# Attention two batches ahead of the output, with two batches in float32 beside the preparation of w_in

## The chip, the core and the metric

The kernel runs on one core of a Trainium2 chip. The metric is the device time of one launch in microseconds (us). A core has five engines that each work through their own queue in order: TensorE (PE; its weight loads are listed apart as PEld), VectorE (DVE), ScalarE (ACT), GpSimd (POOL) and SyncE (SP), which here issues all the DMAs. They wait for one another by semaphores. PE writes only into PSUM, which this kernel cuts into eight banks under the names `psc` (2 tiles of 2 banks), `pm` (3 tiles) and `pav` (1 tile).

## The reference

Sigmoid attention feeds a two-layer network with an ELU between its layers.

```python
# q, k, v: (8, 12, 448, 64) float32; w_in: (768, 2048); w_out: (2048, 768)
S = q.shape[2]
scores = np.matmul(q, k.transpose(0, 1, 3, 2)) / np.sqrt(64) - np.log(S)
attn = 1.0 / (1.0 + np.exp(-scores))
attn_out = np.matmul(attn, v).astype(np.float32)
x = attn_out.transpose(0, 2, 1, 3).reshape(8 * 448, 768)
h = x @ w_in
g = np.where(h > 0.0, h, np.exp(np.minimum(h, 0.0)) - 1.0)
out = (g @ w_out).astype(np.float32)
```

The two weights arrive as 8-byte floats, so that each weight is two 32-bit words.

## The kernel before

**Split numbers.** Most matmuls multiply float32 values that are held as two float16 values, a high part and a low part. `split` (lines 120 to 122) makes them: ACT writes the high part, scaled by a power of two, and DVE subtracts it from the source to get the low part. A product then takes three float16 matmuls: high by high, low by high, high by low. The scale of a tile is found first: DVE reduces the largest magnitude of each partition (`absmax`, line 125), multiplies an identity matrix by it (`dg`, line 105), PE multiplies that by ones to spread it over all partitions (`pb`, line 110), and DVE and POOL turn the result into scales (lines 112 to 114 and 317 to 327). `prepare` makes the reductions and `dg`, its inner `scales` makes `pb` and the scales, and `transposed` makes the splits of q and k (`nat`), of v (`vn`), and the DMA that transposes `nat` into `qk` (line 352). They run as three steps, which the main loop calls `second` (what `prepare_pair` returns) and `third` (what `second` returns).

**Attention.** The work goes batch by batch (8), and in a batch by pairs of heads (6). The class `Pair` holds a pair's four key tiles (three of 128 keys for each of two heads, and a rest tile with 64 keys of both). `scores` multiplies keys by queries into `psc`; `soften` applies the sigmoid on ACT into `sg` and splits it into `at` (ACT line 413, DVE line 414); `values` multiplies by v into `pav`; `finish` splits `pav` into `xh`, the attention output of the pair, and takes its largest magnitude. `EXACT = 1` says that batch 0 does its attention in plain float32: no splits of q, k, v and the sigmoid, but seven PE transposes for each pair (line 337), a copy to `early` (line 341), and float32 matmuls.

**Weights.** w_in is read in 16 tiles. `w_in_tile` finds the power of two of each from its words (ACT lines 138 and 142, DVE lines 143 and 157, sums on PE line 150) and splits it into `wi` (lines 121 and 122). The list `W_IN` says how many tiles have been done after each pair. w_out is read by `load_w_out` in 2 halves of 16 tiles: 16 magnitude steps of a half, then its 16 splits. A part of the staging lies in buffers that attention uses (`at`, `o`). `step` advances this by one tile; `wo` takes the place of the staging of w_in, so that it can start only when all of w_in is split.

**Hidden layer and output.** `hidden(b)` first calls `rescale`, which brings the six pairs of x to one scale (lines 448 to 452: five DVE instructions on whole `xh` tiles), and then `moe1`: 16 groups of 18 matmuls into `ph`, each followed by the exponential on ACT (line 511), the ELU on DVE (513, 514) and a split into `g`. `moe2(b)` multiplies `g` by `wo`: 48 matmuls for each tile of the output, 6 tiles for an even batch and 8 for an odd one (an odd batch also takes the last 64 tokens of the batch before), with a scaled copy `o` on DVE and a DMA out.

**Order.** The part up to and with `hidden(0)` is ordered by a scheduler, which may interleave what it finds ready: batch 0's pairs beside the w_in tiles, then `moe1` of batch 0 beside w_out (`w_out_beside`: four steps for each f from 2). The rest stands under `manual_schedule` for PE, ACT, DVE and SP, in the order of the code: for b = 1 to 7, attention of batch b with the matmuls of `moe2(b - 1)` filled in (`fill`: between the first two and the last two score tiles, and again before `values`), then `hidden(b)`. In pair n the splits of pair n + 1 (`third`) come after its first two softened tiles, the maxima of pair n + 2 (`prepare_pair`) before its last two, and the scales of pair n + 2 (`second`) ahead of `values`. Behind the last `hidden` stands `moe2(7)` alone. ACT changes between the sigmoid's and the exponential's tables once each way in a batch, and manual dependencies keep that so.

Of the kernel before, what the change touches and what calls it, by code (L numbers as in the profile page):

```python
# [32 lines left out]
def attention_ffn(  # L33
# [12 lines left out]
    P = 128  # L46
# [10 lines left out]
    EXACT = 1  # L57
    SP = 4
    SKEW = 2
    W_IN = [1, 3, 6, 9, 12, 15, 16]  # L60
    W_LOAD = [1, 1]
    W_OUT = 4
# [180 lines left out]
    last_exp = {}  # L243
# [123 lines left out]
    class Pair:  # L367
# [23 lines left out]
        def soften(self, g):  # L391
# [6 lines left out]
            if b - 1 in last_exp:  # L398
                tc.add_manual_dep(
                    a.ins,  # L400
                    last_exp[b - 1],
# [41 lines left out]
    def rescale(b, xh, xs):  # L443
# [5 lines left out]
        for c in range(NP - 1):  # L449
            nc.vector.tensor_scalar(xh[:, c], xh[:, c], rr[:, c : c + 1], None, op0=ALU.mult)  # L450
        nc.vector.tensor_tensor(
            xm[:, : NP - 1], xm[:, : NP - 1], rr[:, : NP - 1], op=ALU.mult
        )
        yield
# [24 lines left out]
    def moe1(b, g, xh, m, first, beside=None):  # L479
# [8 lines left out]
        for f in range(NF):  # L488
# [23 lines left out]
            last_exp[b] = a.ins.name  # L512
            nc.vector.tensor_scalar(e, e, 1.0, -1.0, op0=ALU.min, op1=ALU.add)  # L513
# [82 lines left out]
    def prepare_pair(n):  # L596
# [4 lines left out]
        if hp == 0:  # L601
            xh_of[b] = sb.tile([P, NK, 2, S], F16, tag="xh", name=f"xh{b}", bufs=2)
            xs_of[b] = sb.tile([P, 3, NP], F32, tag="xs", name=f"xs{b}", bufs=2)
# [11 lines left out]

    def w_out_beside(f):
        nonlocal wo, steps
        if f == 0:
            w_in_ratios()
            wo = sb.tile([P, NH, NF, 2, HM], F16, tag="wo", name="wo")  # L620
            steps = load_w_out(wo)
        if f >= 2:
            step(W_OUT)
        if f == NF - 1:
            step(1)
# [5 lines left out]
    def hidden(b, beside=None):  # L631
# [3 lines left out]
        next(whole)  # L635
        yield
# [38 lines left out]
    third = prepare_pair(EXACT * NP + 1)()  # L675
# [3 lines left out]
    next(h)  # L679
# [5 lines left out]
    with tc.manual_schedule(engines={E.PE, E.Activation, E.DVE, E.SP}):  # L685
        for b in range(EXACT, B):
            out_scale(*of_moe2, slice(0, 1 if b == EXACT else NH))
            tiles = moe2(b - 1, g, wo)
            left = NF * NH * (NC + (b - 1) % 2)
# [7 lines left out]
            for hp in range(NP):  # L697
                n = b * NP + hp
                share = left // (NP - hp)
                tail = 4 if hp == NP - 1 else 0  # L700
# [4 lines left out]
                third()  # L705
# [15 lines left out]
                fill(share - gap - tail)  # L721
                third = second()
# [3 lines left out]
                fill(tail)  # L726
# [3 lines left out]
        out_scale(*of_moe2)  # L730
        for _ in moe2(B - 1, g, wo):
            pass
# [30 lines left out]
```

## Time and profile before

| | |
|---|---|
| device time, median of 3 runs | 1272.22 us (1271.79 to 1273.72) |
| the profiled execution's own time | 1270.86 us |
| its span, first to last instruction | 1269.1 us |
| PE busy | 1200.2 us (95%), 7246 matmuls |
| DVE busy | 823.4 us (65%), 1872 instructions |
| ACT busy | 671.8 us (53%), 1015 instructions |
| POOL busy | 84.1 us (7%), 319 instructions |
| mean granted TensorE clock | 0.984 |
| HBM read, written | 58.20 MB, 11.01 MB |

The span is what the trace covers. The profiled execution's own time is 1.76 us longer, and it lies 1.36 us below the median of the runs. A busy PE isn't PE at its peak: the matmuls are pipelined and their ends are modelled. In a timeline a row is a run of like instructions: start, time from the first start to the last end, engine, line, operation, output and input tiles, shapes, count, and in brackets the idle time ahead of it with what ended it. Line numbers in all rows are those of the kernel before, unless the changed kernel is named; there most lines are 1 to 21 higher.

### The profile page before, as it was taken

To read this page: it belongs to the slowest core of one execution; us is meant where nothing else is said; L and a number is where in the kernel's file an instruction comes from. 1 tells how busy PE (TensorE), PEld (TensorE's weight loads), DVE (VectorE), ACT (ScalarE), POOL (GpSimd) and SP (SyncE) were. 2 spreads that over 40 slices of the span, in tenths; PEclk is the share of its full clock that TensorE was granted. 3 is DMA by queue.
4 is the path that set the end of the run, shared out by engine and by line. 5 is a ranking of instruction groups with operands and counts; after the bars stand their busy time and mean duration, and the time that the engine had idled before them with its cause. 6 is when DMAs were issued, how large, how long until landed. Compare 5 with 4: busy or idle time off the path is not lost.

```text
span 1269.1 us, 19337 instructions
## 1 busy us (share of the span) xinstructions
PE 1200.2 (95%) x7246; PEld 610.5 (48%) x7246; DVE 823.4 (65%) x1872; ACT 671.8 (53%) x1015; POOL 84.1 (7%) x319
## 2 busy tenths in 40 slices
PE   5979868999999999999999999999999999999998
PEld 2324334445555554545455554545455554455565
DVE  5898989765766557775666646885576656765500
ACT  5867777643655337744555436654565435663400
POOL 0011001100000000010000000010000100100000
PEclk9889979999999999999999999999999999999999
DMA  8937423420233103340144201440034401410000
GB/s 229 281 100 222 126 77 80 100 49 1 60 84 89 37 1 83 89 86 1 37 92 92 50 1 43 105 103 7 1 86 92 92 1 22 106 43 7 1 25 26
DMA packets 213407, 89.76 MB, mean 71 GB/s; under 512 B 177472, under 2 KB 209216, under 8 KB 213312
## 3 DMA queue, kind: packets, MB, share of 16 engines
q1 hardware_dynamic: 213312, 88.51, 28.7%
q8 instruction: 57, 0.93, 0.3%
q14 instruction: 38, 0.31, 0.1%
HBM read 58.20 MB, written 11.01 MB: 55 GB/s over the span
## 4 chain that ended last, share of the span: by engine, by line
PE 78%; ACT 8%; DVE 7%; DMA 3%; issue 2%; SPq 2%; DVEq 0%; POOL 0%; ACTq 0%; POOLq 0%
PE ph L499 31%; PE po L529 25%; PE psc L384 7%; PE pav L433 6%; PE po_r L529 5%; PE pav L425 3%; ACT sg L395 2%; DMA stage<-in_moe_w_in_dram 2%; ACT at L413 1%; SPq L262 1%; PE pb L110 1%; ACT L395 1%; ACT e L511 1%; DVE e L514 1%; DMA so<-in_moe_w_out_dram 1%
## 5 line engine op out<-in xcount | busy, mean ns | idle before, releaser
L499 PE MATMUL ph<-xh,wi 128*128 128x448 f16 x2304 | 442.0, 353 | 6.1 <-DVE xh L122 2.4
L529 PE MATMUL po<-wo,g 128*128 128x384 f16 x2304 | 392.9, 328 | 0.0
L529 PEld LDWEIGHTS <-g 128*128 128x128 f16 x2688 | 257.2, 98 | 198.4 <-issue 36.3
L499 PEld LDWEIGHTS <-wi 128*128 128x128 f16 x2304 | 225.3, 98 | 218.4 <-issue 7.6
L511 ACT ACTIVATE e<-ph,msc 128x448 f32<-128x448 f32 x128 | 80.8, 633 | 211.7 <-PE ph L499 211.6
L414 DVE SCALAR_TENSOR_TENSOR at<-sg,at 128x896 f16<-128x896 f32 x126 | 137.2, 1090 | 84.5 <-ACT at L413 84.5
L395 ACT ACTIVATE sg<-psc,bias,sc 128x896 f32<-128x896 f32 (+1 forms) x168 | 166.6, 992 | 1.7
L513 DVE TENSOR_SCALAR e<-e 128x448 f32<-128x448 f32 x128 | 50.3, 394 | 170.8 <-ACT e L511 170.7
L121 ACT ACTIVATE xh<-pav,sc 128x448 f16<-128x448 f32 x48 | 30.3, 632 | 216.7 <-PE pav L425 216.7
L384 PE MATMUL psc<-qk 64*128 64x448 f16 x1008 | 116.6, 355 | 11.4 <-ACT sg L395 11.4
L413 ACT ACTIVATE at<-sg 128x896 f16<-128x896 f32 x126 | 119.8, 951 | 4.1
L121 ACT ACTIVATE g<-e,msc 128x384 f16<-128x384 f32 (+1 forms) x192 | 96.0, 534 | 6.0 <-DVE e L514 4.3
L122 DVE SCALAR_TENSOR_TENSOR g<-e,msc,g 128x384 f16<-128x384 f32 (+1 forms) x192 | 94.6, 521 | 0.6
L514 DVE SCALAR_TENSOR_TENSOR e<-ph,msc,e 128x448 f32<-128x448 f32 x128 | 87.3, 683 | 4.0
L384 PEld LDWEIGHTS <-qk 64*128 64x128 f16 x1008 | 41.7, 97 | 89.7 <-issue 60.2
L433 PE MATMUL pav<-at,vn 128*64 128x448 f16 x756 | 80.2, 357 | 0.0
L324 POOL TENSOR_SCALAR sc<-pw 128x1 f32<-128x1 f32 x42 | 12.4, 295 | 843.5 <-DVE pw L114 790.9
L529 PE MATMUL po_r<-wo,g 128*128 128x384 f16 x384 | 64.7, 326 | 0.0
L122 DVE SCALAR_TENSOR_TENSOR xh<-pav,sc,xh 128x448 f16<-128x448 f32 x48 | 32.7, 680 | 48.7 <-ACT xh L121 48.7
L433 PEld LDWEIGHTS <-vn 128*64 128x64 f16 x756 | 39.4, 110 | 50.0 <-issue 27.8
L122 DVE SCALAR_TENSOR_TENSOR nat<-raw,sc,nat 128x384 f16<-128x384 f32 (+1 forms) x126 | 59.1, 524 | 0.0
L121 ACT ACTIVATE nat<-raw,sc 128x384 f16<-128x384 f32 (+1 forms) x126 | 58.8, 529 | 0.0
(103 smaller groups left out, 852.7 us busy)
## 6 DMA issues: line engine op xcount, KB each, us to landing
stage<-in_moe_w_in_dram SPq DMA_DIRECT2D x16, 768.0 KB, 6.6
raw<-in_q_dram SPq DMA_DIRECT2D x96, 96.0 KB, 3.1
raw<-in_k_dram SPq DMA_DIRECT2D x96, 96.0 KB, 2.6
rv<-in_v_dram SPq DMA_DIRECT2D x48, 192.0 KB, 2.7
out_dram<-o SPq DMA_DIRECT2D x48, 192.0 KB, 2.1
wo<-in_moe_w_out_dram SPq DMA_DIRECT2D x19, 384.0 KB, 4.1
so<-in_moe_w_out_dram SPq DMA_DIRECT2D x13, 384.0 KB, 4.3
raw<-in_q_dram SPq DMA_DIRECT2D x48, 32.0 KB, 2.4
```

Source lines behind the costliest of these rows:

```text
L121: nc.scalar.mul(hi, src, s)
L122: nc.vector.scalar_tensor_tensor(lo, src, s, hi, op0=ALU.mult, op1=ALU.subtract)
L384: nc.tensor.matmul(psc[:, j, :S] if g < NC else psc[rows[j], 0, :S], kk[rows[j], o], qq[rows[j], :S], start=(n == 0), stop=(n == len(parts ...
L395: a = nc.scalar.activation(sg[:, :nb], psc[:, :nb, :S], AF.Sigmoid, bias=bias, scale=self.s_scale)
L413: nc.scalar.mul(hi, sg, 2.0**ATOP)
L414: nc.vector.scalar_tensor_tensor(lo, sg, 2.0**ATOP, hi, op0=ALU.mult, op1=ALU.subtract)
L433: nc.tensor.matmul(pav[rows[j], :S], vv[i][:, j * NC + g], sg[k][:, j], start=(g == 0 and n == 0), stop=False,)
L499: nc.tensor.matmul(ph[:, :S], wi[:, wj, c, f * P : (f + 1) * P], xh[:, c, xj], start=(n == 0), stop=(n == 3 * NK - 1),)
L511: a = nc.scalar.activation(e, ph[:, :S], AF.Exp, scale=inv)
L513: nc.vector.tensor_scalar(e, e, 1.0, -1.0, op0=ALU.min, op1=ALU.add)
L514: nc.vector.scalar_tensor_tensor(e, ph[:, :S], inv, e, op0=ALU.mult, op1=ALU.max)
L529: nc.tensor.matmul(po[:, :HM], lh(gj, f), wo[:, i, f, wj], start=(n == 0), stop=(n == 3 * NF - 1),)
```

## The change

The kernel now does the attention of batches 0 and 1 in float32, ahead of everything else (`EXACT = 2`), with two w_in tiles for each pair in place of three. The steps of w_out begin in pair 9 of these twelve, three for each pair, and go on with three for each f of `moe1` of batch 0. The ordered part runs from b = 2: attention of batch b with `moe2(b - 2)` filled in, then `hidden(b - 1)`. At the end `moe2(6)`, `hidden(7)` and `moe2(7)` follow without attention beside them.

`rescale` now yields after each of its five tiles, and the loop calls it once in each of the first five pairs of the next batch. In a pair, `second` and `third` are called together after the first two softened tiles, for pair n + 1; the maxima of pair n + 2 are made after the last two softened tiles, where they stood ahead of them. The fill between the score tiles of a batch's first pair is 10 steps (8 before), and the four steps that were kept back to stand behind the last pair are gone. `xs`, a small tile of scales, has three buffers. A manual dependency keeps the exponentials of `moe1(0)` behind the last sigmoid of batch 1.

```diff
-    EXACT = 1
+    EXACT = 2
-    W_IN = [1, 3, 6, 9, 12, 15, 16]
+    W_IN = [1, 3, 5, 7, 9, 11, 13, 15, 16, 16, 16, 16, 16]
+    W_OUT_FROM = 9
-    W_OUT = 4
+    W_OUT = 3
...
-            if b - 1 in last_exp:
+            if b - EXACT in last_exp:
...
         for c in range(NP - 1):
             nc.vector.tensor_scalar(xh[:, c], xh[:, c], rr[:, c : c + 1], None, op0=ALU.mult)
+            yield
...
-        yield
...
+    def w_out_begin():
+        nonlocal wo, steps
+        w_in_ratios()
+        wo = sb.tile([P, NH, NF, 2, HM], F16, tag="wo", name="wo")
+        steps = load_w_out(wo)
+
     def w_out_beside(f):
...
+        step(W_OUT)
...
+        if n == W_OUT_FROM:
+            w_out_begin()
+        if n >= W_OUT_FROM:
+            step(W_OUT)
...
         for b in range(EXACT, B):
...
-            tiles = moe2(b - 1, g, wo)
-            left = NF * NH * (NC + (b - 1) % 2)
+            tiles = moe2(b - 2, g, wo)
+            left = NF * NH * (NC + b % 2)
...
                 share = left // (NP - hp)
-                tail = 4 if hp == NP - 1 else 0
                 p = pair_of(n)
                 for t in range(2):
                     p.scores(t)
                     p.soften(t)
-                third()
+                second()()
...
-                gap = 8 if hp == 0 else 5
+                gap = 10 if hp == 0 else 5
                 fill(gap)
-                second = prepare_pair(n + 2)
                 for t in range(2, NC + 1):
                     p.scores(t)
                     p.soften(t)
+                second = prepare_pair(n + 2)
...
-                if hp == NP - 1:
-                    h = hidden(b)
+                if hp == 0:
+                    h = hidden(b - 1)
+                if hp < NP - 1:
                     next(h)
-                fill(share - gap - tail)
-                third = second()
+                fill(share - gap)
                 for t in range(NC + 1):
                     p.values(t)
                 p.finish()
-                fill(tail)
...
-        out_scale(*of_moe2)
-        for _ in moe2(B - 1, g, wo):
-            pass
+        for b in range(B - 2, B):
+            out_scale(*of_moe2)
+            if b < B - 1:
+                h = hidden(b + 1)
+                for _ in range(NP - 1):
+                    next(h)
+            for _ in moe2(b, g, wo):
+                pass
+            if b < B - 1:
+                of_moe2 = next(h)
```

The order of the built programs shows two places. The first is DVE's queue in a split pair, here the second pair of a batch; `at` is the softened tile, `nat` and `vn` are the splits of the next pair, `mx`, `mt` and `dg` the maxima of the pair after it, and `al`, `pw` and `sc` what is made of `pb`. Before:

```order
L414 SCALAR_TENSOR_TENSOR at_1_3319<-sg_1_3317,at_1_3319 128x896
L122 SCALAR_TENSOR_TENSOR nat_2_3322<-raw_2_2529,sc_2_3266,nat_2_3322 128x384
L122 SCALAR_TENSOR_TENSOR nat_2_3322<-raw_2_2529,sc_2_3266,nat_2_3322 128x128
L122 SCALAR_TENSOR_TENSOR nat_2_3322<-raw_2_2529,sc_2_3266,nat_2_3322 128x384
L122 SCALAR_TENSOR_TENSOR vn_2_3331<-rv_83,sc_2_3266,vn_2_3331 128x384
L125 TENSOR_REDUCE mx_3_3361<-rv_85 128x1
L125 TENSOR_REDUCE mt_3_3363<-raw_3_3149 128x7
L307 TENSOR_REDUCE mx_3_3361<-mt_3_3363 128x2
L310 TENSOR_TENSOR mx_3_3361<-mx_3_3361,mt_3_3363 64x1 x2
L105 TENSOR_SCALAR dg<-eye,mx_3_3361 128x128 x3
L414 SCALAR_TENSOR_TENSOR at_1_3382<-sg_1_3380,at_1_3382 128x896
L537 TENSOR_SCALAR o_1_0_3412<-po_1_0_3244,osc_1613 128x384
```

In the changed kernel the same stretch, from the second `at` of the pair on, reads:

```order
L416 SCALAR_TENSOR_TENSOR at_1_3699<-sg_1_3697,at_1_3699 128x896
L113 TENSOR_REDUCE al<-pb 128x3
L114 TENSOR_SCALAR al<-al 128x3
L115 TENSOR_SCALAR pw_2_3610<-al 128x3
L319 RECIPROCAL sc_2_3708<-pw_2_3610 128x3
L283 TENSOR_TENSOR xs_2802<-xs_2802,pw_2_3610 128x1
L286 RECIPROCAL xs_2802<-xs_2802 128x1
L123 SCALAR_TENSOR_TENSOR nat_2_3717<-raw_2_2928,sc_2_3708,nat_2_3717 128x384
L123 SCALAR_TENSOR_TENSOR nat_2_3717<-raw_2_2928,sc_2_3708,nat_2_3717 128x128
L123 SCALAR_TENSOR_TENSOR nat_2_3717<-raw_2_2928,sc_2_3708,nat_2_3717 128x384
L123 SCALAR_TENSOR_TENSOR vn_2_3726<-rv_83,sc_2_3708,vn_2_3726 128x384
L416 SCALAR_TENSOR_TENSOR at_1_3765<-sg_1_3763,at_1_3765 128x896
```

The chain from `pb` to the scales, which stood behind the third `at` and served the pair after next, now stands between the second `at` and the splits that use it; the maxima, which stood ahead of the third `at`, come behind it.

The second place is ACT's queue where w_out begins. Before, it begins with the exponentials (`e`) of `moe1(0)`; `wo<-so` and `wo<-wo` are magnitude steps:

```order
L511 ACTIVATE e_0_959<-ph_0_930,msc_929 128x448
L511 ACTIVATE e_2_1010<-ph_3_1045,msc_929 128x448
L138 ACTIVATE wo<-so_0_1019 128x384
L138 ACTIVATE wo<-so_1_1026 128x384
L138 ACTIVATE wo<-wo 128x384
L142 ACTIVATE wo<-wo 128x384
L511 ACTIVATE e_0_959<-ph_1_967,msc_929 128x448
```

In the changed kernel it begins among the sigmoids (`sg`) of the ninth float32 pair:

```order
L396 ACTIVATE sg_2_1027<-psc_2_1024,bias 128x896
L396 ACTIVATE sg_2_1035<-psc_2_1032,bias 128x896
L139 ACTIVATE wo<-so_0_1130 128x384
L139 ACTIVATE wo<-so_1_1137 128x384
L396 ACTIVATE sg_2_1042<-psc_2_1039,bias 128x896
L139 ACTIVATE wo<-wo 128x384
L143 ACTIVATE wo<-wo 128x384
L396 ACTIVATE sg_2_1049<-psc_2_1046,bias 128x448
```

Of the 32 magnitude steps of w_out, 21 now stand ahead of the first exponential on ACT; before, none did except three that only read a staged word.

More of the change, by code (lines that the diff above doesn't have):

```diff
@@ L240, in load_w_out @@
                 yield
-    last_exp = {}
+    last_exp, last_sigmoid = {}, {}
     def load_keys(dst, rest, src, b, h0):
@@ L397, in soften @@
             )
-            if b - 1 in last_exp:
+            last_sigmoid[b] = a.ins.name
+            if b - EXACT in last_exp:
                 tc.add_manual_dep(
                     a.ins,
-                    last_exp[b - 1],
+                    last_exp[b - EXACT],
                     mybir.DependencyInfo(
@@ L512, in moe1 @@
             last_exp[b] = a.ins.name
+            if b == 0:
+                tc.add_manual_dep(
+                    a.ins,
+                    last_sigmoid[EXACT - 1],
+                    mybir.DependencyInfo(
+                        mybir.DependencyClass.NoSync, mybir.DependencyReason.DATA
+                    ),
+                    reason="one change of tables",
+                )
             nc.vector.tensor_scalar(e, e, 1.0, -1.0, op0=ALU.min, op1=ALU.add)
@@ L602, in prepare_pair @@
             xh_of[b] = sb.tile([P, NK, 2, S], F16, tag="xh", name=f"xh{b}", bufs=2)
-            xs_of[b] = sb.tile([P, 3, NP], F32, tag="xs", name=f"xs{b}", bufs=2)
+            xs_of[b] = sb.tile([P, 3, NP], F32, tag="xs", name=f"xs{b}", bufs=3)
         scales = prepare(b, hp, *loaded.pop(n), xs_of[b])
@@ L614, in prepare_pair @@
         return second
-    def w_out_beside(f):
[L617 to L625, printed above, removed]
+    def w_out_begin():
[3 more added lines that the diff above has]
+        steps = load_w_out(wo)
+    def w_out_beside(f):
+        step(W_OUT)
     def pair_of(n):
@@ L634, in hidden @@
         whole = rescale(b, xh, xs)
-        next(whole)
-        yield
+        for _ in range(NP - 1):
+            next(whole)
+            yield
         xp, xr, rest = next(whole)
@@ L674, in attention_ffn @@
             w_in_tile(f)
-    third = prepare_pair(EXACT * NP + 1)()
+        if n == W_OUT_FROM:
+            w_out_begin()
+        if n >= W_OUT_FROM:
+            step(W_OUT)
+    second = prepare_pair(EXACT * NP + 1)
     load_pair(EXACT * NP + 2)
@@ L678, in attention_ffn @@
     h = hidden(0, w_out_beside)
-    next(h)
+    for _ in range(NP - 1):
+        next(h)
     of_moe2 = next(h)
@@ L729, in attention_ffn @@
             of_moe2 = next(h)
-        out_scale(*of_moe2)
-        for _ in moe2(B - 1, g, wo):
-            pass
+        for b in range(B - 2, B):
+            out_scale(*of_moe2)
+            if b < B - 1:
+                h = hidden(b + 1)
+                for _ in range(NP - 1):
+                    next(h)
+            for _ in moe2(b, g, wo):
+                pass
+            if b < B - 1:
+                of_moe2 = next(h)
 _INS = ["q", "k", "v", "moe_w_in", "moe_w_out"]
```

## The prediction

> **What bounds the kernel now.** I read the page first: PE is busy 95% of the span. The busy time by stages then shows where it isn't. Columns: stretch in us, its length, busy us of PE, PEld, DVE, ACT and POOL with instruction counts, granted clock, DMA share, GB/s.
>
> ```profile
> 0.00:30.00 30.00, 17.44 (x79) 8.18 (x79) 15.79 (x37) 14.52 (x19) 2.01 (x14) 1.00 0.86 222
> 30.00:94.50 64.50, 52.20 (x262) 19.89 (x262) 58.37 (x149) 49.23 (x63) 5.56 (x16) 0.89 0.68 197
> 94.50:162.50 68.00, 60.92 (x312) 29.85 (x313) 62.61 (x149) 51.01 (x100) 7.06 (x19) 0.97 0.52 162
> 162.50:191.00 28.50, 18.01 (x99) 8.27 (x98) 22.60 (x48) 21.24 (x35) 2.22 (x6) 0.76 0.34 88
> ```
>
> These are the start, batch 0's float32 pairs with w_in, moe1 of batch 0 with w_out, and the first split pair. In the second and third DVE is busy 90% and 92%: DVE sets the pace there, PE has room. In the fourth nothing is: PE stands at 63%.
>
> The PE timeline shows the fourth stretch against a later phase of the same kind (batch 3 beside an even moe2).
>
> ```profile
> 153.52 8.65 PE L499 MATMUL ph<-xh,wi 128*128 128x448 f16 x36
> 162.53 4.06 PE L529 MATMUL po<-wo,g 128*128 128x384 f16 x24
> 187.32 1.89 PE L433 MATMUL pav<-at,vn 128*64 128x448 f16 x18
> 206.38 1.89 PE L433 MATMUL pav<-at,vn 128*64 128x448 f16 x18
> ...
> 480.01 0.76 PE L384 MATMUL psc<-qk 64*64 64x448 f16 x6 [1.03 <-ACT sg L395]
> 486.75 0.32 PE L110 MATMUL pb<-dg,ones 128*128 128x384 bf16 x1 [1.97 <-DVE dg L105]
> 487.00 1.89 PE L433 MATMUL pav<-at,vn 128*64 128x448 f16 x18
> 500.66 1.89 PE L433 MATMUL pav<-at,vn 128*64 128x448 f16 x18
> 555.05 0.32 PE L110 MATMUL pb<-dg,ones 128*128 128x384 bf16 x1 [1.91 <-DVE dg L105]
> ```
>
> The chain in order of time gives what later stages last (start, us).
>
> ```profile
> 421.99 51.09 PE ph L499 x270
> 560.09 3.40 PE ph L499 x18
> 1202.28 23.40 PE po L529 x144
> ```
>
> From 162.5 on the chain is nearly all PE, with waits of 1 to 2 us at a batch's borders. So the sum has two halves: the end of moe1(0), which I call E (162.5 now), and the PE work behind it.
>
> **Term 1: six more float32 pairs, E.** w_in costs DVE three long instructions a tile, and w_out adds to DVE and ACT.
>
> ```profile
> L122 DVE SCALAR_TENSOR_TENSOR wi<-stage,swi,wi 128x768 f16<-128x768 f32 x16 | 16.0, 1012 | 1.5 <-ACT wi L121 1.4
> L143 DVE SCALAR_TENSOR_TENSOR stage<-stage 128x768 uint32<-128x768 uint32 x16 | 15.2, 953 | 7.3 <-ACT stage L142 7.3
> L157 DVE SCALAR_TENSOR_TENSOR stage<-stage 128x768 uint32<-128x768 uint32 x16 | 15.2, 948 | 0.0
> L395 ACT ACTIVATE sg<-psc,bias 128x896 f32<-128x896 f32 (+1 forms) x24 | 21.0, 906 | 2.1 <-PE psc L384 2.1
> L138 ACT ACTIVATE wo<-wo 128x384 f32<-128x384 f32 x17 | 9.4, 550 | 7.6 <-DMA wo<-in_moe_w_out_dram 7.6
> L121 ACT ACTIVATE wo<-wo,swo 128x384 f16<-128x384 f32 x28 | 16.1, 608 | 2.8 <-DVE wo L122 2.2 <-DVE swo L237 0.7
> ```
>
> The quoted middle fields are a group's busy us and one instruction's ns. DVE was busy 15.79 + 58.37 = 74.2 us up to 94.5. The w_in groups took 46.4 of it, which leaves 27.8 for six pairs, 4.6 each (the tiles' small instructions counted with the pairs, so rather too much). All 16 tiles now lie beside pairs 0 to 7: 46.4 + 8 x 4.6 = 83.5, less the 15.8 done by 30.0, is 67.7. At the share of now, 90%, that is 75 us; I take 74, since the pairs hold fewer small instructions. Pair 7 ends near 104.
>
> PE must not be slower there. A dense run shows what a float32 group of four records takes from start to start:
>
> ```profile
> 35.89 0.97 PE L384 MATMUL psc<-early 64*64 64x448 f32 x4
> 36.78 0.97 PE L433 MATMUL pav<-sg,rv 128*64 128x448 f32 x4
> 37.69 0.98 PE L337 MATMUL pt<-ident,raw 128*128 128x128 f32 x7
> ```
>
> That is 0.9 us, and a pair has four such groups of scores, three of values, one of the rest and its transposes: 8.0 us, below DVE's 67.7 / 7 = 9.7. A split pair needs less PE (term 3 prices it), so moving a batch into float32 adds PE work, but where PE had room.
>
> Pairs 8 to 11 have no w_in, but 21 of the 32 magnitude steps of w_out and five of its splits. ACT: 4 x 21.0 / 6 for sigmoids, 4 x 0.61 for `xh` (a row below), 21 x 2 x 0.55, 5 x 0.61: 43 us. DMA: 18 tiles of 384 KB (three more are staged long before) and four pairs of q, k and v (q two of 96 KB and one of 32, k and v as much) are 9.8 MB, at the 235 GB/s of the stretch in which w_out is loaded now 42 us.
>
> ```profile
> 100.00:120.00 20.00, 19.46 (x107) 9.75 (x105) 17.59 (x43) 15.26 (x30) 3.90 (x7) 1.00 0.80 235
> wo<-in_moe_w_out_dram SPq DMA_DIRECT2D x19, 384.0 KB, 4.1
> raw<-in_q_dram SPq DMA_DIRECT2D x96, 96.0 KB, 3.1
> raw<-in_q_dram SPq DMA_DIRECT2D x48, 32.0 KB, 2.4
> ```
>
> Both give 43; pair 11 ends near 147. The Trainium skill, DMA: Bandwidth & Descriptors, section Bandwidth, puts the limit from HBM for one core at about 358 GB/s; by that the loads would take an estimated 27 us and ACT alone would set these pairs. No row here shows such a rate over a whole stage; the share of 0.80 beside 235 leaves room for it.
>
> moe1(0) takes 3.40 + 51.09 = 54.5 us where nothing disturbs it. It took 68.0 here under w_out's load. With 21 of the magnitudes gone I take 57: the sums of w_out on PE and small waits. E = 147 + 57 = 204, so **+41.5**. Lower bound: all of this front part keeps DVE's pace, 30.0 + (58.37 + 62.61 + 6 x 4.6) / 0.91 = 193. Upper: below, E = 217.
>
> **Term 2: the late start of the split pairs.** E to first values was 187.32 - 162.53 = 24.8; in the later phase it is 487.00 - 473.08 = 13.9. The next spacing was 19.1 against 13.7. The 16.3 us lost came from w_out: its last tiles arrived late and held the `at` buffers, then its last splits stood in DVE's queue. Now the steps start some 40 us further ahead of E; the 16 splits of the second half still stand in the first three pairs, twelve of them in the first at 0.6, as before. Between nothing and 16.3 I take 6, nearest to those splits: **-10**.
>
> **Term 3: one batch of split attention goes.** An even phase, from the end of moe1 to the next, is 560.09 - 473.08 = 87.0. In its place moe2(6) runs alone: 2 x 23.40 = 46.8, by the row of moe2(7). **-40.2**. The other phases keep their number: three even, three odd.
>
> **Term 4: the moved steps in the ordered part.** The waits for `dg` fall: 1.9 at the last pair of each of the two even phases left, -3.8; the wait of 1.0 for the sigmoid goes with the longer first fill, about -1. What is next? The chain from `pb` now lies inside the pair. Rows of one pair now, DVE, POOL, ACT, SP and PE:
>
> ```profile
> 495.64 1.41 DVE L122 SCALAR_TENSOR_TENSOR nat<-raw,sc,nat 128x384 f16<-128x384 f32 x3
> 501.79 0.55 DVE L112 TENSOR_REDUCE al<-pb 128x3 f32<-128x384 f32 x1
> ...
> 503.27 0.23 POOL L319 TENSOR_SCALAR sc<-sc 128x3 f32<-128x3 f32 x1
> ...
> 494.51 1.40 ACT L121 ACTIVATE nat<-raw,sc 128x384 f16<-128x384 f32 x3
> 503.54 0.64 ACT L121 ACTIVATE xh<-pav,sc 128x448 f16<-128x448 f32 x1 [4.54 <-PE pav L425]
> ...
> 497.11 1.57 SPq L352 DMA_TRANSPOSE qk<-nat  x1
> ...
> 503.43 1.31 PE L384 MATMUL psc<-qk 64*128 64x448 f16 x12
> ...
> qk<-nat SPq DMA_TRANSPOSE x42, 4.0
> ...
> L450 DVE TENSOR_SCALAR xh<-xh,rr 128x896 f16<-128x896 f16 x40 | 15.2, 448 | 0.2
> ```
>
> From `al` to POOL's scale is 503.50 - 501.79 = 1.7 us. Started at 495.6, behind the second `at`, it ends at 497.35, so ACT's `nat` begins 2.9 later than 494.51. Behind it on ACT stand `vn`, two sigmoids and an `at`; ACT's idle 4.54 us ahead of `xh` covers that. DVE's `nat` ends near 499.5 in place of 497.05; SP issues the transpose then and lands it 4.0 later, near 503.6, where PE wants it at 503.43. On SP the loads and the output behind the transpose move by the same 2.5 us, which nothing waits for. So PE waits 0.3 in each even-phase pair after a batch's first, 15 in all: +4.5. In odd phases a pair has 16 us and nothing is late. At moe1's start one pb waits for DVE's maxima: six times 0.4, +2.4. Sum **+2**; bounds: -4 (chain hidden) and +14 (0.8 more a pair). The five rescale instructions move beside five pairs, 0.45 each, into DVE's idle time, and POOL's queue only changes its place.
>
> **Sum.** 41.5 - 10 - 40.2 + 2 = -6.7: 1270.86 - 6.7 = 1264.2 for the profiled execution, 1.36 more for the median: **1265.5 us**. About 0.2% (2.5 us) is what a measurement of this kernel can tell from no change.
>
> **Rivals.** (a) *The float32 pairs keep their spacing; slower.* Now it is 12.0 us, (88.40 - 28.52) / 5:
>
> ```profile
> 28.52 0.61 ACT L121 ACTIVATE xh<-pav,sc 128x448 f16<-128x448 f32 x1
> 88.40 0.61 ACT L121 ACTIVATE xh<-pav,sc 128x448 f16<-128x448 f32 x1
> ```
>
> With DVE 9.7, ACT near 10 and PE 8.0 at once, in-order queues may wait for each other and hold it there. Then E = 28.5 + 11 x 12.0 + 56.5 = 217, term 1 is +54.5, and the time 1278.5. It decides from a spacing of 11.4 (E = 211), where the gain is gone. For it: PE's granted clock of 0.89 in this stage; against: DVE's work per pair falls by a tile. The Trainium skill, TensorE: Matmul & The Clock Gate, What's actually happening, says that an idle window of about 3.4 us halves PE's clock; the 0.89 with PE busy 81% agrees, and a longer stage of that kind would keep paying. Chance 0.18.
>
> (b) *The wait only changes its place.* The transpose, 2.5 us later, bounds every even pair by 1 us and the first ones by 3: term 4 becomes +14, the time 1277.5. For it: 0.2 us of margin in my own sum; against: ACT's idle 4.54. It decides from 0.5 a pair. Chance 0.10.
>
> (c) *The front fills better.* DMA isn't the limit, DVE's pace holds, and w_out leaves no backlog: E = 195, term 2 -14: time 1252.5. For it: DMA share 0.80; against: three engines near 90% at once. Chance 0.14.
>
> (d) *The parts cancel.* E = 208, the backlog stays at 8: 1271.5. Chance 0.13.
>
> The forecast keeps 0.45, for 1259 to 1269.5. **Numbers.** Faster: all of the forecast and (c): 0.59, less 0.01 for its upper edge: 0.58. Same: (d) 0.13 and parts of (a) and (b) 0.07: 0.20. Slower: the rest of these, 0.21, and that edge: 0.22. The range takes in (d), (b) and most of (a) above and the upper half of (c) below: 1253 to 1280.
>
> **What would show it.** Right: moe1(0) ends between 199 and 209; float32 pairs spaced 10 to 10.8; DVE busy near 90% up to pair 7; ACT's waits for w_out's DMAs small; first values 14 to 20 us after E; even phases near 86 us with no wait for `dg` at their last pair. Wrong: E above 211; PE waiting for the `qk` transpose by over 0.5 us a pair; w_out's magnitudes waiting on ACT in front of sigmoids.

## The result, and the profile after

The changed kernel is slower: 1288.47 us in the median against 1272.15 us of the kernel before beside it, a ratio of 1.0125 (95% interval 1.0105 to 1.0145). The forecast was 1265.5 us with a range up to 1280; rival (a) had come out at 1278.5. The profiled execution took 1288.24 us, its span is 1286.5 us, 17.4 more than before. (Three runs lie between 1288.24 and 1288.58 us; a fourth, at 1403.14 us, was disturbed and is left out of the ratio.)

The busy time by stages of the changed kernel, with the columns as before (stretch, length, PE, PEld, DVE, ACT and POOL busy us, granted clock, DMA share, GB/s). The stages are the start, pairs 1 to 7 with w_in, pairs 8 to 11 with w_out, and `moe1` of batch 0 up to the first `po`:

```profile
0.00:30.00 30.00, 17.46 (x79) 8.20 (x79) 15.79 (x37) 14.67 (x19) 2.00 (x14) 1.00 0.87 222
30.00:116.00 86.00, 67.39 (x338) 25.85 (x340) 66.53 (x168) 58.42 (x74) 4.33 (x20) 0.92 0.60 168
116.00:165.10 49.10, 40.07 (x183) 14.25 (x181) 37.24 (x97) 35.50 (x62) 2.00 (x7) 1.00 0.62 193
165.10:224.30 59.20, 54.94 (x290) 27.09 (x288) 49.86 (x105) 39.92 (x74) 4.01 (x9) 1.00 0.33 93
```

In the second row DVE is busy 66.53 of 86.00 us, 77%; in the stage that answers to it before it was 90%. PE has 78%, ACT 68%, the DMAs 60%. Over the whole stage no engine is near full, and still pair 7 comes 12 us behind the forecast (116 for 104). The averages hide one thing: the DMAs are full in the first part and nearly idle late.

```profile
30.00:45.00 15.00, 12.02 (x58) 4.38 (x58) 12.08 (x30) 12.63 (x18) 0.51 (x3) 0.89 0.98 288
...
90.00:105.00 15.00, 10.86 (x43) 3.69 (x43) 12.15 (x39) 6.21 (x9) 1.29 (x7) 0.77 0.15 34
```

How far the pairs lie apart is read from the rows in which ACT begins a pair's `xh` (start, us, engine, line). These are pairs 0, 7, 8 and 11:

```profile
28.35 0.61 ACT L122 ACTIVATE xh<-pav,sc 128x448 f16<-128x448 f32 x1
...
115.81 0.63 ACT L122 ACTIVATE xh<-pav,sc 128x448 f16<-128x448 f32 x1 [2.37 <-PE pav L427]
127.50 0.62 ACT L122 ACTIVATE xh<-pav,sc 128x448 f16<-128x448 f32 x1
...
165.11 0.61 ACT L122 ACTIVATE xh<-pav,sc 128x448 f16<-128x448 f32 x1
```

The first two steps, with the DMAs nearly full, are 11.8 and 12.0 us, and the next five 12.8, 13.3, 13.6, 15.3 and 8.8, so the DMAs' rate alone doesn't make them. Eleven steps in 136.8 us are 12.4 us each, against 12.0 before with three w_in tiles a pair in place of two, and 10.8 in the forecast (118.6 / 11).

PE's timeline where the front ends, and then the long rows of the chain of waits in order of time:

```profile
224.31 1.95 PE L540 MATMUL po<-wo,g 128*128 128x384 f16 x11 [0.69 <-DVE e L525]
233.84 1.32 PE L435 MATMUL pav<-at,vn 128*64 128x448 f16 x12
```

```profile
323.14 51.09 PE ph L501 x270
476.08 51.09 PE ph L501 x270
619.25 51.09 PE ph L501 x270
772.20 51.09 PE ph L501 x270
914.37 51.09 PE ph L501 x270
1067.15 51.08 PE ph L501 x270
...
1118.23 46.80 PE po L540 x288
1168.49 51.08 PE ph L501 x270
```

E is 224.3 in place of 162.5. From there to the first long `ph` row it is 98.8 us; before it was 269.27 - 162.53 = 106.7. From start to start the long rows are then 152.9, 143.2, 153.0, 142.2 and 152.8 us apart, and 101.3 to the last, with `moe2(6)` alone in it for 46.80. Before they were, from the same rows of its chain, 152.7, 141.6, 152.7, 143.2, 152.7 and 139.1. The first split pair's values now begin 9.5 us behind E and end 17.9 behind it, against 24.8 and 26.7 before. So the 17.4 us are +61.8 in the front, -7.9 in the first split batch, and -36.5 in the rest (1286.5 - 323.1 against 1269.1 - 269.3).

The waits of the front, from 25 to 162 us, that mattered most in the runs below (engine and line, what it waited for: us in all, times, longest; SPq is SP's DMA queue):

```profile
SPq L248 <- PE pav L435: 34.1, 9, 9.8
```

```profile
PE pav L435 <- ACT sg L396: 17.5, 12, 3.5
...
ACT xh L122 <- PE pav L427: 12.7, 8, 3.9
ACT sg L396 <- PE psc L385: 8.6, 11, 2.7
DVE mx L126 <- DMA rv<-in_v_dram: 8.3, 6, 2.4
```

PE waits for sigmoids, ACT for PE's values and scores, DVE for loads of v, and those loads for PE: the engines wait in a ring, and no single wait of the three engines in these rows is longer than 3.9 us.

### The profile page after: what moved, and what is told of

The parts are those of the page before. It is cut to its first block, busy times and chain, and to the rows that moved or that the text cites. A ratio compares the mean times of both kernels' runs of the same rounds, so it can differ in the third digit from the quotient of the medians.

```text
span 1286.5 us, 19071 instructions
## 1 busy us (share of the span) xinstructions
PE 1215.2 (94%) x7204; PEld 617.0 (48%) x7204; DVE 794.4 (62%) x1794; ACT 643.6 (50%) x971; POOL 84.7 (7%) x289
## 4 chain that ended last, share of the span: by engine, by line
PE 66%; ACT 12%; DVE 9%; DMA 6%; issue 3%; SPq 2%; POOL 1%; DVEq 0%; ACTq 0%; POOLq 0%
PE ph L501 31%; PE po L540 19%; PE po_r L540 5%; PE psc L385 5%; ACT sg L396 4%; PE pav L435 4%; ACT at L415 3%; DMA stage<-in_moe_w_in_dram 2%; PE pav L427 2%; DVE at L416 2%; DMA so<-in_moe_w_out_dram 1%; ACT nat L122 1%; DVE mt L126 1%; DMA wo<-in_moe_w_out_dram 1%; DVE mx L126 1%
## 5 line engine op out<-in xcount | busy, mean ns | idle before, releaser
L540 PE MATMUL po<-wo,g 128*128 128x384 f16 x2304 | 387.2, 326 | 0.7 <-DVE e L525 0.7
L416 DVE SCALAR_TENSOR_TENSOR at<-sg,at 128x896 f16<-128x896 f32 x108 | 117.7, 1090 | 89.2 <-ACT at L415 89.1
L396 ACT ACTIVATE sg<-psc,bias,sc 128x896 f32<-128x896 f32 (+1 forms) x144 | 142.7, 991 | 2.7 <-PE psc L385 1.4
L385 PE MATMUL psc<-qk 64*128 64x448 f16 (+1 forms) x864 | 101.4, 358 | 3.2 <-ACT sg L396 2.4
L415 ACT ACTIVATE at<-sg 128x896 f16<-128x896 f32 x108 | 102.5, 950 | 3.3
L122 ACT ACTIVATE nat<-raw,sc 128x384 f16<-128x384 f32 (+1 forms) x108 | 51.0, 533 | 96.1 <-POOL sc L320 95.0
L123 DVE SCALAR_TENSOR_TENSOR g<-e,msc,g 128x384 f16<-128x384 f32 (+1 forms) x192 | 94.5, 521 | 5.0 <-ACT g L122 4.4
L435 PE MATMUL pav<-at,vn 128*64 128x448 f16 x648 | 73.8, 358 | 15.8 <-ACT at L415 11.4
L548 DVE TENSOR_SCALAR o<-po,osc 128x384 f32<-128x384 f32 x48 | 29.4, 613 | 78.8 <-PE po L540 71.6
L385 PEld LDWEIGHTS <-qk 64*128 64x128 f16 (+1 forms) x864 | 35.8, 98 | 71.9 <-issue 41.0
L435 PE MATMUL pav<-sg,rv 128*64 128x448 f32 x144 | 37.4, 607 | 23.0 <-ACT sg L396 21.0
```

Of the source, the lines that this page charges most:

```text
L122: nc.scalar.mul(hi, src, s)
L123: nc.vector.scalar_tensor_tensor(lo, src, s, hi, op0=ALU.mult, op1=ALU.subtract)
L385: nc.tensor.matmul(psc[:, j, :S] if g < NC else psc[rows[j], 0, :S], kk[rows[j], o], qq[rows[j], :S], start=(n == 0), stop=(n == len(parts ...
L396: a = nc.scalar.activation(sg[:, :nb], psc[:, :nb, :S], AF.Sigmoid, bias=bias, scale=self.s_scale)
L415: nc.scalar.mul(hi, sg, 2.0**ATOP)
L416: nc.vector.scalar_tensor_tensor(lo, sg, 2.0**ATOP, hi, op0=ALU.mult, op1=ALU.subtract)
```

## The experiments

Theories. **A**: a float32 pair's own chain (transposes, `early`, scores, sigmoids through two `psc` tiles) is as long as 12 us. **B**: the weights' instructions stand between the pair's own in the queues of ACT and DVE. **C**: loads of v wait for values, since there are two `rv` tiles, and loads behind them wait too. **D**: the moved steps of the ordered part cost more than the +2 of term 4. All edits are to the changed kernel unless the kernel before is named. Ratios are to the kernel before, run on the same chip.

**1. Bare pairs** (label `bare`).

```diff
...
-            load_w_in(1)
-            w_in_tile(f)
-        if n == W_OUT_FROM:
-            w_out_begin()
-        if n >= W_OUT_FROM:
-            step(W_OUT)
+            nc.gpsimd.memset(wi[:, :, :, f * P : (f + 1) * P], 1.0)
+        if n == EXACT * NP - 1:
+            nc.gpsimd.tensor_copy(stage[0][:, 0, 0:1], xs_of[1][:, 2, NP - 1 :])
+            w_out_begin()
```

> The changed kernel with the work on w_in left out (wi and its scales are filled with ones, w_in isn't read) and all w_out steps held back until the last float32 pair is done: the twelve float32 pairs run bare. It leaves out part of the computation, and only the spacing of the pairs is read. In the changed kernel they were 12.4 us apart. Theory A (their own chain: the transposes of the next pair share two psc tiles with the scores, so that transposes, copy to early, scores and sigmoids follow one another): the spacing stays at 10.5 us or more with nothing beside it. Theory B (the weights' instructions stand between a pair's own on ACT and DVE): it falls to 8.0 to 9.3 us, near the 8.0 us of PE work. Theory C (a load of v waits for the values of two pairs ahead, since there are two rv tiles, and the loads behind it wait too): 10.5 to 12 us, with DVE's maxima waiting for rv.

ACT's rows of pairs 0, 1 and 7, and the busy time from 45 to 100 us:

```profile
35.40 0.64 ACT L122 ACTIVATE xh<-pav,sc 128x448 f16<-128x448 f32 x1 [2.52 <-POOL sc L288]
43.59 0.64 ACT L122 ACTIVATE xh<-pav,sc 128x448 f16<-128x448 f32 x1 [1.93 <-PE pav L427]
...
97.68 0.63 ACT L122 ACTIVATE xh<-pav,sc 128x448 f16<-128x448 f32 x1 [1.93 <-PE pav L427]
```

```profile
45.00:100.00 55.00, 49.80 (x232) 17.51 (x232) 27.83 (x70) 26.00 (x32) 1.44 (x7) 1.00 0.33 78
```

Most steps are 9.0 us, and PE is busy 91% of the time. So a bare pair is bound by PE, 1 us above the 8.0 us that the prediction counted, and A and C fall as sole causes: the pair's own chain and the two `rv` tiles are all still there. The weights' work, in whatever way, costs 3.4 us a pair. With bare pairs throughout, and the last stage as it was in the changed kernel, E would be 28.4 + 11 x 9.0 + 59.2 = 187, so the weights beside the pairs cost 37 us of it.

**2. A third tile for v** (`v3`).

```diff
+    third_rv = sb.tile([P, 2 * NC + 2, D], F32, tag="nat", name="rv2")
...
-        rv = rvs[(b * NP + hp) % len(rvs)]
+        n = b * NP + hp
+        rv = third_rv if n < EXACT * NP and n % 3 == 1 else rvs[n % 3 // 2 if n < EXACT * NP else n % 2]
```

> The changed kernel with a third rv tile for the float32 pairs (it lies in the room of nat, which they don't use). Theory C: the waits of SP for PE's values and of DVE's maxima for rv go, the spacing falls to 11.5 us or less and the time by 8 us or more, to 1280 us or below. Theories A and B: those waits go too, but something else comes last; the spacing stays within 0.4 us of 12.4 and the time between 1285 and 1291 us.

Measured: 1282.08 us, ratio 1.0077 (1.0054 to 1.0100). The wait of the row that stood at 34.1 us:

```profile
SPq L251 <- PE pav L439: 15.5, 5, 6.7
```

Pairs 0 to 10 lie 11.3 us apart, (142.7 - 29.3) / 10, but pair 11 follows only 16.1 us behind, and the time falls by some 6 us in place of 8. C holds for about 1 us a pair and isn't the whole.

**3. Transposes out of `psc`** (`pt_pm`).

```diff
-                pt = ps.tile([P, 2, 512], F32, tag="psc", name=f"pt{u}", bufs=2)
...
+                for i, n_t in ((0, 4), (4, 3)):
+                    pt = ps.tile([P, 512], F32, tag="pm", name=f"pt{u}_{i}", bufs=3)
...
```

> The changed kernel with the float32 pairs' transposes written in two pm tiles of one bank in place of one psc tile of two, and copied to early in two parts; nothing else is changed. Theory A: the scores of a pair no longer share their two tiles with the transposes of the next, the spacing falls to 10.5 us or less, E to about 203, the time to 1265 to 1272 us. Theories B and C: the transposes move ahead, but the spacing stays above 12 us and the time between 1284 and 1292 us.

Measured: 1299.03 us, ratio 1.0202 (1.0185 to 1.0219): slower than any theory said. The pairs came closer, 11.4 us up to pair 10, (146.2 - 31.9) / 10, but pair 11's `xh` begins 27.4 us behind pair 10's. ACT's rows in pair 11 show why; between its second and third sigmoid stand steps of w_out and of the next pair, and the first of them waits for its load:

```profile
155.04 1.01 ACT L397 ACTIVATE sg<-psc,bias 128x896 f32<-128x896 f32 x1 [0.49 <-PE psc L386]
160.28 0.56 ACT L139 ACTIVATE wo<-wo 128x384 f32<-128x384 f32 x1 [4.24 <-DMA wo<-in_moe_w_out_dram]
...
165.88 1.52 ACT L397 ACTIVATE sg<-psc,bias 128x896 f32<-128x896 f32 x2
```

That is theory B, seen in one place: an in-order queue with a sigmoid behind an instruction that waits for a DMA. The prediction had named it ("w_out's magnitudes waiting on ACT in front of sigmoids") as a sign that it was wrong.

**4. Three w_in tiles a pair** (`w_in3`).

```diff
-    W_IN = [1, 3, 5, 7, 9, 11, 13, 15, 16, 16, 16, 16, 16]
+    W_IN = [1, 3, 6, 9, 12, 15, 16, 16, 16, 16, 16, 16, 16]
```

> The changed kernel with three w_in tiles beside a pair in place of two; w_out still begins in pair 9. Bare, the pairs were 9.0 us apart, with two tiles 12.4, in the kernel before with three 12.0. Theory B1 (each tile costs its share): pairs with three tiles are 14 us apart, those behind them 9; E stays within 3 us and the time between 1285 and 1291 us. Theory B2 (it is the presence of the weights' instructions in the queues, not their number): three tiles keep 12.0 to 12.6 us, two pairs become bare, E falls by 6 to 9 us and the time to 1279 to 1283 us.

Measured: 1291.09 us, ratio 1.0143 (1.0125 to 1.0162), no better than the changed kernel. Neither theory holds as written: pairs with three tiles lie 12.3 us apart, (99.9 - 50.7) / 4, as B2 has it, and the next two 7.9 and 10.7; but then those with w_out take 12.9, 13.7 and 15.8, pair 11 comes at 161.0, 4.1 earlier, and `moe1` of batch 0 ends at 220.1 in place of 220.6. What the front does not pay in one pair it pays in another.

**5. The front in an order by hand** (`hand_front`): the scheduler replaced by `manual_schedule` for the twelve pairs, on top of the edits of 2, 3 and 8.

```diff
...
+        for n in range(EXACT * NP):
+            loaded[n + 2] = load_qk(*pairs[n + 2]), load_v(*pairs[n + 2])
+            if last:
+                last.finish()
+            p.scores(1)
+            p.soften(1)
+            if exact:
+                transposes(n + 1)
+            beside()
+            p.values(0)
...
+            if exact:
+                third()
+                ahead = pair_of(n + 1)
+                ahead.scores(0)
+                ahead.soften(0)
+            beside()
+            p.values(3)
+            last, p = p, ahead
...
```

> The changed kernel with the float32 pairs in an order written out by hand: the sigmoid of the next score tile stands ahead of the weights' instructions on ACT, one step of w_in (half a tile) or w_out stands in each of a pair's four places, PE's sums come a step behind, the loads of w_out go out two steps ahead, the transposes lie in pm, three rv tiles; the old order within the split pairs. If the spacing of 12.4 us comes from the order of the queues (theory B): the pairs are 10 to 10.8 us apart, E comes to 197 to 207, and the time is 1252 to 1266 us. If it comes from the engines' work itself with three of them near full, whatever the order: the spacing stays above 11.3 us and the time above 1268 us.

One of w_out's 32 staged tiles is overwritten here before its signs are read, so that its values differ; the instructions are as many. Measured: 1283.87 us, ratio 1.0092 (1.0074 to 1.0109). Up to pair 6 the spacing is 12.6 us, (103.83 - 28.37) / 6, more even than before but no shorter. The busy time of those pairs, and their waits:

```profile
30.00:104.00 74.00, 55.33 (x293) 21.09 (x293) 64.93 (x155) 53.02 (x65) 7.68 (x19) 1.00 0.67 177
```

```profile
PE si L205 <- DVE stage L196: 11.6, 12, 1.6
ACT wi L125 <- DVE stage L161: 9.4, 13, 1.1
PE pav L509 <- DVE xh L126: 7.3, 6, 1.7
DVE wi L126 <- ACT wi L125: 7.3, 11, 1.1
```

PE no longer waits for sigmoids. DVE is busy 88%, with 11 us in a pair (64.93 / 74 x 12.6), and the other engines wait for it. That is more of DVE's time than the 9.6 us of the changed kernel (66.53 / 86 x 12.4), with the copies to `early` in two parts among it. So this order doesn't bring the spacing down, but it raises DVE's own share of a pair too: that the scheduler's order makes the 12.4 us is neither borne out nor excluded. This order is one of many, and what the best one would give isn't shown. The clock is 1.00 here and 0.92 in the changed kernel, at nearly the same spacing, so a full clock alone doesn't bring the pairs closer. What it costs the changed kernel isn't shown; an estimate from 67.39 us of PE at 0.92 is some 5 us of the 86 (67.39 x 0.08). The rule named beside rival (a) (the Trainium skill, TensorE: Matmul & The Clock Gate, What's actually happening) asks for an idle window of some 3.4 us. Here PE idles 25% of the stage, never longer than 1.7 us at a time, and keeps its clock, which agrees; but in the changed kernel's stage PE's longest gap is 2.45 us, and the clock falls all the same, to 0.77 from 90 to 105. So the rule, read as one unbroken gap, is not what these traces show.

**6. What lies beside a pair, part by part** (`w_loads`, `w_act`, `w_dve`, `w_both`): the bare kernel with w_in's loads put back, and in the last three a part of the work on each tile.

```diff
+    def part_of_tile(f):
...
# w_loads
+        nc.gpsimd.memset(d, 1.0)
+        nc.gpsimd.tensor_copy(wm[:, 0:1], hi[:, 0, 0:1])
# w_act
+        nc.scalar.activation(t, h, AF.Abs, scale=2.0**-112)
+        nc.scalar.activation(lo, top, AF.Copy, scale=2.0**-13, bias=2.0**-14 - 0.5)
+        nc.scalar.mul(d[:, 0], t, 2.0**WTOP)
# w_dve
+        nc.vector.scalar_tensor_tensor(
+            u, hi, 0x3F000000, lo, op0=ALU.bitwise_and, op1=ALU.bitwise_and
+        )
+        signed(t, hi)
+        nc.vector.scalar_tensor_tensor(
+            d[:, 1], t, 2.0**WTOP, d[:, 0], op0=ALU.mult, op1=ALU.subtract
+        )
# w_both: the lines of w_act, and those of w_dve on a tile of their own
```

> The run with bare pairs, with w_in's loads put back (GpSimd reads one word of each tile so that the staging turns over; wi stays filled with ones). It leaves out the work on w_in; only the pairs' spacing up to pair 7 is read, against 9.0 us bare and 12.4 us in the changed kernel. If the loads are what spreads the pairs (by SP's queue, where a load of v waits for values of two pairs before and w_in's loads stand behind it, or by traffic): 10.5 us or more. If not: 8.8 to 9.4 us.

> As the run with the loads, and ACT's three instructions a w_in tile put back, without DVE's (no waits between the two; the values are not w_in's). Two tiles put 5.4 us of ACT beside a pair's 4.1. If sigmoids that stand behind these instructions set the spacing: 11 us or more. If ACT has room in a pair: 9.0 to 9.8 us.

> As the run with the loads, and DVE's three long instructions a w_in tile put back, without ACT's. Two tiles put 5.8 us of DVE beside a pair's own. If the copy to early and the split of pav, which stand behind these instructions, set the spacing: 11 us or more. If DVE has room: 9.0 to 9.8 us. If neither this run nor the one with ACT's comes above 10 us, the spacing of 12.4 us is made by the two together: waits of ACT for DVE and back, one tile after the other.

> As the run with the loads, with ACT's three and DVE's three instructions a w_in tile both put back, but on data of their own, so that neither engine waits for the other within a tile (it leaves out part of the work on w_in). Pair 7's xh began 63 us behind pair 0's bare (62.3), 71.6 with the loads alone, 78.5 with ACT's part, 75.4 with DVE's part, and 87.5 in the changed kernel. If the parts add up in the queues: 84 to 88 us. If the waits between ACT and DVE make the rest: 75 to 80 us.

Rows of pairs 0 and 7, for the loads alone, ACT's part, DVE's part, and both without waits between them:

```profile
33.98 0.63 ACT L122 ACTIVATE xh<-pav,sc 128x448 f16<-128x448 f32 x1 [2.27 <-PE pav L436]
...
105.57 0.63 ACT L122 ACTIVATE xh<-pav,sc 128x448 f16<-128x448 f32 x1 [1.93 <-PE pav L436]
```

```profile
28.11 0.63 ACT L122 ACTIVATE xh<-pav,sc 128x448 f16<-128x448 f32 x1 [0.62 <-PE pav L438]
...
106.59 0.63 ACT L122 ACTIVATE xh<-pav,sc 128x448 f16<-128x448 f32 x1 [1.93 <-PE pav L438]
```

```profile
26.25 0.63 ACT L122 ACTIVATE xh<-pav,sc 128x448 f16<-128x448 f32 x1 [2.74 <-PE pav L442]
...
101.63 0.63 ACT L122 ACTIVATE xh<-pav,sc 128x448 f16<-128x448 f32 x1 [1.93 <-PE pav L442]
```

```profile
27.50 0.62 ACT L122 ACTIVATE xh<-pav,sc 128x448 f16<-128x448 f32 x1
...
109.13 0.63 ACT L122 ACTIVATE xh<-pav,sc 128x448 f16<-128x448 f32 x1 [1.93 <-PE pav L445]
```

From pair 0 to pair 7: 62.3 us bare, 71.6 with the loads, 78.5 with ACT's part, 75.4 with DVE's, 81.6 with both, 87.5 in the changed kernel. The last run falls between its two expectations. So of the 25.2 us that the pairs lose, the loads make about 9, the two engines' instructions without waits another 10, and about 6 are left for what `w_both` still lacks: the waits of ACT and DVE for each other, six sums a tile on PE, DVE's small instructions. These parts weren't told apart further, and each number is one execution (bare and with the loads alone, pair 0 starts some 6 us later, for a reason given at the end, and has a part of its loads behind it).

The scheduler also takes this work ahead: the last tile is done by 72 us with ACT's part, 79 with DVE's and 74 with both, and from there most steps are about 9 us, while in the changed kernel the work lasts until 119. So the totals up to pair 7 compare, and the single steps don't. With the loads alone the slow steps are 10.9, 11.7 and 14.0 us, from 51 to 88. The DMAs' share is 1.03 from 45 to 60 us, 0.95 from 60 to 75 and 0.66 from 75 to 90, and DVE's maxima wait for loads of v (the second row is from 45 to 100 us):

```profile
45.00:60.00 15.00, 12.67 (x61) 4.18 (x58) 4.04 (x11) 7.04 (x10) 0.90 (x5) 1.00 1.03 306
```

```profile
DVE mx L126 <- DMA rv<-in_v_dram: 16.3, 6, 6.3
```

**7. The order within a split pair, in the kernel before** (`before_order`).

```diff
...
-                third()
+                second()()
...
-                second = prepare_pair(n + 2)
                 for t in range(2, NC + 1):
                     p.scores(t)
                     p.soften(t)
+                second = prepare_pair(n + 2)
...
-                third = second()
```

> The kernel before with the new order within a pair alone: second and third together behind the first two softened tiles, the maxima behind the last two. It prices term 4 by itself. By the prediction's working: four even phases lose a wait for dg of 1.9 us each (-7.6), twenty pairs wait 0.3 us each for the transpose (+6), seven starts of moe1 wait 0.4 us more for the maxima (+2.8): +1, a time of 1271 to 1275 us. If the transpose bounds these pairs by 1 us (rival b): +15, about 1287 us. If the new order costs nothing in the pairs: -5 to -7, about 1266 us.

Measured: 1290.57 us, ratio 1.0141 (1.0120 to 1.0162): rival (b)'s size. Its even phases are 145.1, 145.3 and 142.2, the odd ones 153.4 each, and the first `ph` row begins at 276.54 in place of 269.27. Of these 7.3 us, 4.7 stand ahead of E (167.21 for 162.53), where no split pair runs yet; so of the 18.1 us by the spans some 13.4 lie in the split batches. The waits from 300 to 1150 us are now these (PEld is PE's weight load, here the first of a pair's scores):

```profile
PE pav L433 <- ACT at L413: 7.4, 5, 1.6
...
PE pav L433 <- DVE at L414: 3.4, 8, 0.6
PE pb L110 <- DVE dg L105: 3.0, 14, 0.3
```

```profile
PEld L384 <- DMA qk<-nat: 12.7, 17, 1.2
```

In the kernel before, the same stretch had 9.7 us of `pb` waiting for `dg` in five waits, and none for the transpose. The wait has changed its place, as the rival says: the transpose is late by 0.75 us a time (the changed kernel has 10.5 us in 14 such waits in the same stretch), and values wait for `at`, which now stands behind the splits.

**8. The old order in the changed kernel** (`after_old`): the edit of 7 backwards.

```diff
...
-                second()()
+                third()
...
                 fill(gap)
+                second = prepare_pair(n + 2)
...
-                second = prepare_pair(n + 2)
...
                 fill(share - gap)
+                third = second()
```

> The changed kernel with the order within a split pair put back (third behind the first two softened tiles, the maxima ahead of the last two, second ahead of values); the longer first fill and the spread rescale stay. If the new order costs here what it cost in the kernel before (2.9 us an even phase, 0.7 an odd one, 5.1 in the first split phase): -10 to -14, a time of 1275 to 1279 us. If the spread rescale and the longer fill pay most of it back, as the phases of the changed kernel suggest (even phases 142.7 against 141.3): -2 to -6, 1282 to 1287 us. The front does not change: E stays at 224.

Measured: 1282.02 us, ratio 1.0065 (1.0052 to 1.0078), 6.4 us below the changed kernel; its even phases are 141.2 both, the odd ones 152.4, 152.4 and 152.1. By the two spans it is 9.2 us: 1.0 up to E (223.31), 3.4 from there to the first long `ph` row (318.73), and the rest in the phases. D holds, and more mildly here than in the kernel before.

**9. `second` behind `values`** (`before_behind`, and with the third tile for v `behind_v3`), both in the kernel before.

```diff
-                third = second()
                 for t in range(NC + 1):
                     p.values(t)
+                third = second()
```

> The kernel before with second put behind values in place of ahead of them, so that pb no longer waits for dg in front of the values (these waits were 11.6 us in all). If the waits are simply lost time: -6 to -11, a time of 1261 to 1267 us. If the chain from pb to the splits is late instead, as in the run with the new order: no gain or a loss, 1271 us or more.

> The kernel before with second behind values and a third rv tile for its six float32 pairs. In the changed kernel the third tile took 1 us from each pair's spacing and 6 us from the time. If that holds for six pairs: E falls by 4 to 6 us and the time to 1258 to 1262 us. If moe1 of batch 0 is held by w_out's loads instead, E stays, and the time at 1263 to 1267 us.

Measured: 1264.90 us, ratio 0.9937 (0.9925 to 0.9950), and 1263.85 us, ratio 0.9929 (0.9911 to 0.9948). The wait for `dg` is gone from PE's list from 300 to 1150 us; what stands there is smaller:

```profile
PE psc L384 <- ACT sg L395: 6.7, 6, 1.2
PE pav L433 <- DVE at L414: 6.5, 5, 1.3
```

Even phases are 139.9, 139.9 and 138.1. So the waits for `dg` were lost time, but the change removed them at the price of others. The third tile adds nothing that can be measured here: `moe1` of batch 0 ends 5.7 us later in its trace, and the first split batch takes most of it back.

**10. The changed kernel, mended** (`after_best`): the edits of 2, 8 and 9 together.

> The changed kernel with the old order within a split pair, second behind values, and three rv tiles. The order gave -6.4 us, the third tile -6.4, second behind values gave the kernel before -8.7 over four even phases, of which two are left here. If the gains add: -6.4 - 6.4 - 3 = -16, a time of 1271 to 1274 us, no better than the kernel before and 8 us or more behind that kernel with second behind values. If two batches ahead can pay once these losses are gone: below 1264 us.

Measured: 1263.95 us, ratio 0.9934 (0.9921 to 0.9948). Some long rows of its chain:

```profile
309.56 51.09 PE ph L505 x270
461.35 51.09 PE ph L505 x270
599.78 51.09 PE ph L505 x270
```

The first comes 13.6 us earlier than in the changed kernel, the phases are 151.8 (odd) and 138.4 (even), against 152.7 and 139.3 with the same order in the kernel before; the gains came to 24.5 us where I had added up 16. It beats both kernels, and lies level with the kernel before when that has `second` behind `values` (ratios 0.9934 and 0.9937): two batches ahead win nothing over that here.

## Why the prediction was wrong, point by point

**Term 1 failed**: +61.8 in place of +41.5, which is 20.3 of the 24.1 us by which the change in span was off (-6.7 forecast, +17.4 measured). Some 12 of them lie up to pair 7, 6 in pairs 8 to 11, and 2 in the last stage. The work was counted well: the forecast had 67.7 us of DVE up to pair 7, and 66.5 were done between 30 and 116. The step that failed is "At the share of now, 90%, that is 75 us": the share was 77%, and pair 7's `xh` began at 115.8, not near 104. A busy share is an outcome of how several engines meet in a stage, and this stage met differently: a third less weight work on DVE a pair, and a pair that takes 9.0 us with nothing beside it, with loads, ACT and DVE each adding to it. It wasn't a steady share in the kernel before, either: there the DMAs stood at 0.97 from 30 to 60 us and at 0.43 from 60 to 94.5. The same holds for pairs 8 to 11, with 43 forecast from sums of ACT's and the DMAs' work and 49.3 measured. `moe1` of batch 0 came near: 55.5 us to its last `ph` and 3.7 to the first `po`, 59.2 in all, for 57.

**Rival (a)** was the one that happened: 12.0 us of spacing named, 12.4 measured, "in-order queues may wait for each other" as its reason, and a chance of 0.18. How much of the 12.4 is order and how much the clock isn't told apart. Its E, 217, was too low by 0.4 us a pair and 2.7 in the last stage. The row that should have raised its chance stood in the prediction: the pairs were 12.0 apart with three tiles, and nothing in the trace had shown that one tile less brings them closer. In the run with three tiles they are 12.3 apart, so one tile less doesn't; the pairs with one tile or none beside them are the shorter ones there.

**Term 2** held: -10 forecast; from E to the first long `ph` row -7.9. The late start is where it came from: the first pair's values end 8.8 us nearer to E. Of the 8.4 us left of the 16.3, 3.4 are the new order's, by `after_old`.

**Term 3** held: `moe2(6)` alone took 46.80 us, and the mean even phase of before was 141.3; 101.3 - 141.3 is -40.0, for -40.2.

**Term 4** came out near its sum, for partly other reasons. Two even phases are 1.4 us longer than the mean before, three odd ones 0.2: +3.4, for +2. But the order alone costs more than this, 6 to 9 us in this kernel and 18 in the kernel before (13 behind E). The prediction's working, that the waits for `dg` fall by 3.8 us and the transpose costs 0.3 us a pair, is right about the kinds of wait and too kind about their sizes (0.75 us each). Why the order costs less in the changed kernel stays open. With the old order its phases are 141.2 and 152.4, against 141.3 and 152.7 in the kernel before, so the spread `rescale` and the longer first fill win little by themselves; that they soften the new order is possible, but no run took one of them alone.

**The sum** of terms 2 to 4 was -48.2 and is -44.4. Six pairs of attention were worth 40 us where they were, and would have to cost less than that at the front. From the last pair's `xh` to E the changed kernel takes 59.2 us, the kernel before 162.53 - 88.40 = 74.1, so that having less of w_in's and w_out's work behind the last pair paid back 14.9. The steps from pair to pair came to 136.8 us in place of 59.9: 76.9 for six more pairs, where six bare pairs would take 54. The forecast had 118.6 - 59.9 = 58.7, so it was in effect the case in which the six pairs are added nearly bare and the weights cost the pairs no more than they did.

## What to carry to other kernels

Do not carry an engine's busy share from one stage to a stage with another mix: ask first how long the moved work takes alone (here 9.0 us a pair), and take it as the floor. Here three engines and the DMAs stood at 60 to 80% over the stage, and work put beside other work still added a part of its length on each engine, even though none of them was full on average; a share over a long stage can also hide a part in which one of them is. And a wait on PE was better removed here by putting the waiting instruction behind work that is ready (-8 us) than by moving the chain that it waits for (+18).

## What the runs showed of the hardware

In the bare run GpSimd fills `wi` in a row, and DVE's queue stands still meanwhile: a copy of 128x128 elements takes 21 us, against 0.23 us in the changed kernel.

```profile
1.69 21.21 DVE L91 CAST eye<-ident 128x128 bf16<-128x128 f32 x1 [0.20 <-POOL ident masks.py:199]
...
2.96 19.86 POOL L683 MEMSET wi<- 128x1536 f16 x15
```

The Trainium skill, SBUF — State Buffer, section SBUF: two separate sides, describes a lock that GpSimd and some of DVE's instructions share, held for a whole instruction. The trace fits one blocking the other, but DVE waited for a whole row of fills, not for the one under way; that it is this lock isn't shown. The stop is the likely reason why pair 0 comes at 35.4 us there, and at 28.4 in the changed kernel. The other surprise was the DMAs: loads alone, with nothing computed from them, spread the pairs by 9 us in seven. These loads ran at 306 GB/s and a share of 1.03 from 45 to 60 us, and the changed kernel's at 288 GB/s and 0.98 from 30 to 45; so for this mix of loads the DMAs are full near 300 GB/s.
